# Modulation in two column halves, keys and queries side by side, and four V tiles in the first block of a transformer layer

## The chip, the cores and the metric

The kernel runs on one core of a Trainium2 chip. The metric is the device time of one execution in microseconds; the kernel before takes 1766.52 us, the median of three runs (1766.45 to 1767.83). A core has five engines that run side by side, each through its own list of instructions in order: TensorE (PE, with its weight loads shown as PEld), VectorE (DVE), ScalarE (ACT), GpSimd (POOL) and SyncE (SP), which here only issues DMAs. They wait for each other through semaphores.

## The reference

One transformer layer with conditional modulation, in fp32, for 2048 tokens of width 512:

```
mod = silu(c) @ w_mod                      # six vectors of 512: sa, ca, ga, sb, cb, gb
h   = layernorm(x) * (1 + ca) + sa
q, k, v = h @ wqkv                         # 32 heads of 16
x   = x + ga * (softmax(q k^T / 4) v @ wo)
h   = layernorm(x) * (1 + cb) + sb
x   = x + gb * (gelu(h @ w1 + b1) @ w2 + b2)
```

The inner width of the last step is 1792. Only the beginning matters here: the vectors `ca` and `sa`, the first layer norm, and the projections of its output to keys, queries and values.

## The kernel before

**Numbers in two parts.** Each fp32 operand of a projection is split into a high part, rounded to the format in which TensorE runs fast, and a low part, the remainder. A product is three matmuls per chunk of 128 features: high by high, low by high, high by low. A tile of 512 output columns over four chunks is therefore 12 matmuls, all into one PSUM bank (`mm3`, L294).

**Blocks.** The 2048 tokens are four blocks of 512. For each block b the loop at L534 gives out, in this order: the layer-norm statistics of block b+1 (`ln1`, L271), the load of x for block b+2, the key projection of head group 0 (`proj_qk`, L307), the normalisation of the rows of block b+1 (L278, DVE), the query projection, then some V tiles (`proj_v`, L354), the transposes of block b+1 with their evacuation (`ln1_t`, L284; `transposed`, L252), more V tiles, and in blocks 0 and 1 two further modulation vectors (`mod_rows`, L205). `V_A` (L47) says how many V tiles stand before and behind the transposes: 1 and 2 in block 0, 1 and 1 in block 1, 0 and 1 in block 2. The remaining ten V tiles and all other head groups follow behind the blocks, then attention, then the feed-forward part. There is no planner: the order of each engine's work is the order in which the Python code gives it out.

**Evacuating the transposes.** The transposed normalised x of a chunk lies in PSUM as 128 features by 512 tokens. ACT scales and shifts it by two columns of `modc` (one plus `ca`, and `sa`, per feature; L262) into an fp32 tile, DVE rounds that to `hi` (L263), and DVE or POOL, in turn, subtracts to get `lo` (L264).

**Before the first block.** SP loads c, the four tiles of x of block 0, two 1 MB tables of `w_mod` (for `ca` and `sa`), the weights of the first keys and queries, the V weights, x of block 1 and the second group's weights, in this order. PE first runs 22 throwaway matmuls on an identity matrix (`keep_warm`, L509, `NWARM`); then `mod_part` (L200) multiplies silu(c) with the first table, the chunks of x are transposed, the second table is multiplied, five throwaway matmuls follow, and `mod_cols` (L216) turns the row of 512 values (copied from PSUM by ACT, `mod_copy`) into columns, by four matmuls of two columns each, from which DVE writes `modc`. Only then can the evacuation begin. `split_w` (L164) splits the weights: those of group 0 on DVE with one subtraction on POOL, the V weights on ACT with subtractions in turn on DVE and POOL. POOL sets the constant columns of five V staging tiles (L503 to L505) right behind the layer norm's power of -0.5 (L241).

**Pairs of blocks.** In odd blocks the keys of the two last blocks are also added and subtracted (L330, DVE), rounded (L331, ACT) and their remainders taken on POOL (L346).

**PSUM.** Eight banks are dealt out from three rings: `mx` (three banks), `sc` (four) and `pv` (one). A bank can be dealt again once its last reader is done.

Of the kernel before, what the change touches and what calls it, by code (L numbers as in the profile page):

```python
# [7 lines left out]
F32 = mybir.dt.float32  # L8
# [8 lines left out]
P = 128  # L17
# [35 lines left out]
def block_kernel(ctx: ExitStack, tc: tile.TileContext, x, wqkv, wo, w1, b1, w2, b2, c, w_mod, out):  # L53
# [78 lines left out]
    sel_b = apool.tile([P, 2, P], F32, name="sel_b")  # L132
    ones = apool.tile([P, 2 * S // P], F32, name="ones")
    gp.memset(ones, 1.0)

    wm_r = w_mod.rearrange("(k p) n -> p k n", p=P)

    def load_wm(i, slot):
        sy.dma_start(halves[1][slot], wm_r[:, :, i * D : (i + 1) * D])
        return halves[1][slot]  # L140

    def x_tile(b, t):
# [10 lines left out]
    def load_w(k):  # L153
# [7 lines left out]
                sy.dma_start(raw[:, i], wq_r[:, i, 2 * D :])  # L161
        raws[k] = raw

    def split_w(k):  # L164
        raw = raws.pop(k)
        if k < 4:
            t = wslots[k % 2].rearrange("p a (b n) -> p (a b) n", n=P).rearrange("p (h w k) n -> p h w k n", h=2, w=2)
            for w in (1, 0):
                if k == 0:
                    ve.tensor_copy(t[:, 0, w], raw[:, w])  # L170
                elif k > 1:
                    gp.tensor_copy(t[:, 0, w], raw[:, w])
                else:
                    ac.activation(t[:, 0, w], raw[:, w], AF.Copy)
                eng = ve if k == 0 and w else gp
                eng.tensor_tensor(t[:, 1, w], raw[:, w], t[:, 0, w].bitcast(F32), op=ALU.subtract)
            w_hi[k], w_lo[k] = t[:, 0], t[:, 1]
        else:
            w_hi[k], w_lo[k] = vslots
            for i in range(KC):  # L180
                ac.activation(w_hi[k][:, i], raw[:, i], AF.Copy)
                eng = gp if i % 2 else ve
                eng.tensor_tensor(w_lo[k][:, i], raw[:, i], w_hi[k][:, i].bitcast(F32), op=ALU.subtract)

    sy.dma_start(c_c, c.rearrange("a (k p) -> p (a k)", p=P))
    load_x(0)
    wms = [load_wm(1, 0), load_wm(0, 1)]
    load_w(0)


    ac.activation(s_c, c_c, AF.Exp, scale=-1.0)
# [8 lines left out]
    def mod_part(ps, i, wm):  # L200

        for k in range(KC):
            te.matmul(ps[32 * k : 32 * (k + 1)], s_m[:, i, k], wm[:, k], start=i == 0, stop=i == 1)

    def mod_rows(wms):  # L205
        ps = bank()
# [1 line left out]
            mod_part(ps, i, wms[i])  # L208
        return mod_copy(ps)

    def mod_copy(ps):
        r = apool.tile([P, D], F32, tag="h32", name="mrow", bufs=3)
        ac.activation(r, ps, AF.Copy)
        return r

    def mod_cols(v, r):  # L216

        ps = bank()
        for fc in range(KC):
            te.matmul(ps[:, fc * 2 : fc * 2 + 2], r[:, fc * P : (fc + 1) * P], sel[:, :2], start=True, stop=True)  # L220
        p2 = ps[:, : 2 * KC].rearrange("p (f i) -> p f i", i=2)
        ve.tensor_scalar(modc[:, v, :, 0], p2[:, :, 0], 1.0, None, op0=ALU.add)
        ve.tensor_copy(modc[:, v, :, 1], p2[:, :, 1])

    def mod_store(r):

# [77 lines left out]

    st = [ac]

    def proj_qk(b, k, w, fill=()):  # L307
        hi, lo = hT[b]
        ps = bank()
        mm3(ps, [w_hi[k][:, w, i] for i in range(KC)], [w_lo[k][:, w, i] for i in range(KC)],  # L310
            [hi[:, i] for i in range(KC)], [lo[:, i] for i in range(KC)], fill)
        parts = tpool.tile([P, 2, TB], FR, tag="parts", name="parts", bufs=5)
        pair = w and k < 2
        if k or pair and b % 2 == 0:
            raw = tpool.tile([P, TB], F32, tag="raw", name="raw", bufs=3)
            ac.activation(raw, ps, AF.Copy)
            if pair:
                k2[b % 2] = raw
        if k:
            gp.tensor_copy(parts[:, 0], raw)  # L320
            gp.tensor_tensor(parts[:, 1], raw, parts[:, 0].bitcast(F32), op=ALU.subtract)
        else:
            ac.activation(parts[:, 0], ps, AF.Copy)
            ve.tensor_tensor(parts[:, 1], ps, parts[:, 0].bitcast(F32), op=ALU.subtract)
        if pair and b % 2:
            pm = [tpool.tile([P, TB], F32, tag="pm", name="pm", bufs=1), k2[0]]
            pmh = [tpool.tile([P, 2, TB], FR, tag="parts", name="pmh", bufs=5) for _ in range(2)]
            if not k:
                for i, op in enumerate((ALU.add, ALU.subtract)):
                    ve.tensor_tensor(pm[i], ps, k2[0], op=op)  # L330
                    ac.activation(pmh[i][:, 0], pm[i], AF.Copy)  # L331

        def pair_store():
            for i in range(2):
                t0 = (b - 1 + i) * TB
                st[0].dma_start(kpm_d[k][:, :, t0 : t0 + TB].rearrange("a p t -> p a t"), pmh[i].bitcast(F32))

        def rest():
            st[0].dma_start(qk_d[w][k][:, :, b * TB : (b + 1) * TB].rearrange("a p t -> p a t"), parts.bitcast(F32))
            if pair and b % 2:  # L340
                for i, op in enumerate((ALU.add, ALU.subtract)):
                    if k:
                        gp.tensor_tensor(pm[i], k2[1], k2[0], op=op)
                        gp.tensor_copy(pmh[i][:, 0], pm[i])
                    eng = ve if not k and b == NB - 1 else gp
                    eng.tensor_tensor(pmh[i][:, 1], pm[i], pmh[i][:, 0].bitcast(F32), op=ALU.subtract)  # L346
# [7 lines left out]
    def proj_v(b, t, fill=()):  # L354
        hi, lo = hT[b]
        ps = bank()
        sl = slice(t * P, (t + 1) * P)
        mm3(ps, [hi[:, i, sl] for i in range(KC)], [lo[:, i, sl] for i in range(KC)],
            [w_hi[4][:, i] for i in range(KC)], [w_lo[4][:, i] for i in range(KC)], fill, late_b=False)
# [134 lines left out]
        return [] if left[u] else [max_rows(u)]  # L494


    load_w(4)
    load_x(1)
    load_w(1)
    sy.dma_start(one_d.rearrange("a (p f) -> (a p) f", p=P // 2), ones)  # L500
    xn = ln1(0)()
    for t in vst:
        gp.memset(t[:, :, 4 * VW :], 0.0)  # L503
        for j in range(4):
            gp.memset(t[:, :, j * VW + DH], 1.0)  # L505
    split_w(0)
    warm = bank_pv()

    def keep_warm(n):  # L509
        for i in range(n):  # L510
            te.matmul(warm[:, :P], ident, ident, start=True, stop=True)

    keep_warm(NWARM)
    ps = bank()
    mod_part(ps, 0, wms[0])
    ev = ln1_t(0, xn, lambda: mod_part(ps, 1, wms[1]))
    mrow = mod_copy(ps)
    keep_warm(5)
    mod_cols(0, mrow)
    ev()  # L520
    split_w(4)
    wms = [load_wm(4, 0), load_wm(3, 1)]
    mrow = None
    vitems = [(b, t) for b in range(NB) for t in range(4)]
# [9 lines left out]
    for b in range(NB):  # L534
        if b == NB - 1:
            close(lcm)
            kcm, kpool = pool("kpool")
            kts = [kpool.tile([P, 2, S], FR, name=f"kt{i}") for i in range(2)]
            qmcm, qmpool = pool("qmpool")
            kpm[0], kpm[1] = kts  # L540
            load_qm(0)
        if b + 1 < NB:
            rows = ln1(b + 1)
        if b + 2 < NB:
            load_x(b + 2)
        proj(proj_qk, b, 0, 1)
        if b == NB - 1:
            st[0] = sy
            rest()
            rest, st[0] = lambda: None, ac  # L550
            build_k(kts[0], kpm_d[0], 0, 0, 2 * TB)
            split_w(1)
            load_w(2)
        else:
# [470 lines left out]
```

## Time and profile before

| | |
|---|---|
| median of three runs | 1766.52 us (1766.45 to 1767.83) |
| profiled execution | 1765.35 us, span 1763.6 us |
| PE busy | 1748.7 us, 99% of the span |
| DVE, ACT, POOL busy | 1404.5, 1355.8, 320.1 us |
| mean granted clock of TensorE | 0.998 |
| DMA traffic | 144.17 MB, mean 82 GB/s |

The profile is one execution. Its times are microseconds from the first instruction. A timeline line shows start, duration, engine, source line, operation, output and inputs by the program's names, shapes and the number of instructions put together; in square brackets the idle time of the engine before it, and what ended it. An fp32 matmul appears as two records, a transpose as one. "PEclk" is the share of its full clock that TensorE was granted. A line of the windows view has the stretch, its length, then the busy time and number of instructions of PE, PEld, DVE, ACT and POOL, the granted clock, the share of the DMA engines that was busy, and GB/s.

### The profile page before, as it was taken

To read this page: it belongs to the slowest core of one execution; us is meant where nothing else is said; L and a number is where in the kernel's file an instruction comes from. 1 tells how busy PE (TensorE), PEld (TensorE's weight loads), DVE (VectorE), ACT (ScalarE), POOL (GpSimd) and SP (SyncE) were. 2 spreads that over 40 slices of the span, in tenths; PEclk is the share of its full clock that TensorE was granted. 3 is DMA by queue.
4 is the path that set the end of the run, shared out by engine and by line. 5 is a ranking of instruction groups with operands and counts; after the bars stand their busy time and mean duration, and the time that the engine had idled before them with its cause. 6 is when DMAs were issued, how large, how long until landed. Compare 5 with 4: busy or idle time off the path is not lost.

```text
span 1763.6 us, 29164 instructions
## 1 busy us (share of the span) xinstructions
PE 1748.7 (99%) x10554; PEld 901.1 (51%) x10554; DVE 1404.5 (80%) x2553; ACT 1355.8 (77%) x2580; POOL 320.1 (18%) x347
## 2 busy tenths in 40 slices
PE   8999999999999999999999999999999999999998
PEld 6755555344343443343343343343433478788887
DVE  6579999898888888888888888888886286838453
ACT  3478888999999999999999999999999732213222
POOL 3204422010000000000000000000003154636462
PEclk9999999999999999999999999999999999999999
DMA  8767636811500411411410101101013064423341
GB/s 277 250 141 163 151 115 130 130 37 29 87 23 23 82 27 23 74 36 23 74 35 24 38 25 33 38 23 36 23 60 104 22 195 131 126 78 114 102 120 48
DMA packets 124100, 144.17 MB, mean 82 GB/s; under 512 B 38930, under 2 KB 72722, under 8 KB 122004
## 3 DMA queue, kind: packets, MB, share of 16 engines
q1 hardware_dynamic: 120644, 135.55, 30.9%
q10 hardware_dynamic: 3312, 6.76, 1.0%
q8 instruction: 83, 1.36, 0.3%
q14 instruction: 61, 0.50, 0.1%
HBM read 106.37 MB, written 35.87 MB: 81 GB/s over the span
## 4 chain that ended last, share of the span: by engine, by line
PE 93%; DVE 3%; DMA 1%; issue 1%; POOL 1%; SPq 0%; ACT 0%; ACTq 0%; DVEq 0%; POOLq 0%
PE pv L693 29%; PE mx L429 19%; PE sc L300 16%; PE sc L860 13%; PE mx L447 6%; PE mx L924 5%; PE pv L924 2%; PE sc L800 1%; PE mx L800 1%; DMA wmod<-in_w_mod_dram 1%; DVE glo L907 0%; POOL w2l L731 0%; DMA rb<-rden 0%; PE sc L257 0%; DVE mxs L431 0%
## 5 line engine op out<-in xcount | busy, mean ns | idle before, releaser
L861 ACT ACTIVATE p<-sc 128x512 f32<-128x512 f32 x2048 | 1054.8, 615 | 39.4 <-PE sc L860 13.4
L431 DVE TENSOR_REDUCE mxs<-mx 128x1 f32<-128x512 f32 x1472 | 927.5, 684 | 112.9 <-PE sc L860 76.6
L693 PE MATMUL pv<-p,vg 128*32 128x512 f32 x4096 | 546.0, 605 | 0.0
L860 PE MATMUL sc<-qst,kq 50*128 50x512 f32 x1024 | 284.1, 435 | 0.0
L860 PE MATMUL sc<-qst,kt 50*128 50x512 f32 x1024 | 282.3, 431 | 0.0
L429 PE MATMUL mx<-kq,qmx 48*128 48x512 f32 x768 | 262.1, 428 | 0.2
L429 PE MATMUL mx<-kt,qmx 48*128 48x512 f32 x704 | 240.3, 428 | 0.1
L429 PEld LDWEIGHTS mx<-kq,qmx 48*128 48x128 f32 x768 | 122.6, 184 | 228.5 <-DVE mxs L431 209.2
L903 ACT ACTIVATE g<-sc,b_c 128x512 f32<-128x512 f32 x56 | 38.6, 690 | 237.2 <-PE sc L300 233.1
L429 PEld LDWEIGHTS mx<-kt,qmx 48*128 48x128 f32 x704 | 113.3, 184 | 208.8 <-DVE mxs L431 191.1
L458 DVE CUSTOM_DVE_ANT_0 cp<-mx,cp 128x512 f32<-128x512 f32 x288 | 187.2, 688 | 36.3 <-PE mx L447 31.3
L471 POOL CAST m<-mn 128x16 fp32r<-128x16 f32 x32 | 6.3, 197 | 1026.0 <-DVE mn L465 1026.0
L454 ACT ACTIVATE cp<-mx 128x512 f32<-128x512 f32 x288 | 156.3, 597 | 38.8 <-PE mx L447 38.4
L693 PEld LDWEIGHTS pv<-p,vg 128*32 128x32 f32 x4096 | 81.1, 108 | 180.7 <-issue 169.3
L860 PEld LDWEIGHTS sc<-qst,kq 50*128 50x128 f32 x1024 | 125.5, 185 | 32.1 <-ACT p L861 23.6
L907 DVE TENSOR_TENSOR glo<-g,ghi 128x512 fp32r<-128x512 f32 x56 | 60.1, 1073 | 94.8 <-ACT ghi L906 94.8
L860 PEld LDWEIGHTS sc<-qst,kt 50*128 50x128 f32 x1024 | 125.5, 185 | 10.1 <-ACT p L861 3.1
L447 PE MATMUL mx<-kt,qmx 48*128 48x512 f32 x576 | 113.4, 455 | 0.0
L729 POOL TENSOR_TENSOR w1l<-w1r,w1h 128x512 fp32r<-128x512 f32 x56 | 76.8, 1372 | 152.7 <-DVE w1h L728 130.5
L447 PEld LDWEIGHTS mx<-kt,qmx 48*128 48x128 f32 x576 | 58.3, 184 | 56.4 <-issue 33.4
L300 PE MATMUL sc<-hThi,w 128*128 128x512 f32 x256 | 84.0, 436 | 2.2 <-DVE hThi L263 2.2
L731 POOL TENSOR_TENSOR w2l<-w2r,w2h 128x512 fp32r<-128x512 f32 x56 | 81.1, 1448 | 6.6 <-DVE w2h L730 6.2
(158 smaller groups left out, 1671.4 us busy)
## 6 DMA issues: line engine op xcount, KB each, us to landing
w1r<-in_B_w_dram SPq DMA_DIRECT2D x56, 256.0 KB
w2r<-in_B_w_dram SPq DMA_DIRECT2D x56, 256.0 KB
qk<-parts SPq DMA_DIRECT2D x25, 512.0 KB
qmx<-qk SPq DMA_DIRECT2D x192, 64.0 KB
qst<-qk SPq DMA_DIRECT2D x192, 64.0 KB
wmod<-in_w_mod_dram SPq DMA_DIRECT2D x6, 1024.0 KB
kq<-qk SPq DMA_DIRECT2D x24, 256.0 KB
kt<-qk SPq DMA_DIRECT2D x24, 256.0 KB
```

What stands on the lines that cost most here:

```text
L300: te.matmul(ps, p, q, start=i == 0, stop=i == len(terms) - 1)
L429: te.matmul(ps, qmx[u][rows, p, qc * P : (qc + 1) * P], kst[u // NB][rows, p, kr * TB : (kr + 1) * TB], start=True, stop=True)
L431: ve.tensor_reduce(mxs[u][:, p, a, qc, kr : kr + 1], ps, axis=AX.X, op=ALU.max, negate=True)
L447: te.matmul(ps, qmx[u][rows, p, qc * P : (qc + 1) * P], kpm[u // NB][rows, p, t0 : t0 + TB], start=True, stop=True)
L454: ac.activation(vabs[n, a], ps, AF.Abs)
L458: ve.tensor_tensor_reduce(v, ps, v, -0.5, 3.0e38, ALU.add, ALU.min, mxs[u][:, p, a, qc, r : r + 1])
L693: te.matmul(cur_pv[0][32 * j : 32 * (j + 1)], vg[g][:, kc, j * VW : j * VW + 32], pt.pop((s, j)), start=kc == 0, stop=kc == NKC - 1)
L729: gp.tensor_tensor(alo, a, ahi.bitcast(F32), op=ALU.subtract)
L731: gp.tensor_tensor(blo, b, bhi.bitcast(F32), op=ALU.subtract)
L860: te.matmul(ps, k[r0 : r0 + KX, p, kc * P : (kc + 1) * P], q[r0 : r0 + KX, p], start=True, stop=True)
L861: ac.activation(pb, ps, AF.Exp, scale=SCALE)
L924: te.matmul(acc[qb][t], p[:, sl], q, start=f == 0 and n == 0, stop=f == NF - 1 and n == 2)
```

## The change

A function `first_block` takes the place of the code before the loop and of block 0's two projections.

- Each of the two `w_mod` tables is loaded in two halves of 256 columns: first halves, then the first key and query weights, then second halves. The load of the second group's weights (`load_w(1)`) goes from the start into block 1.
- `mod_part`, `mod_copy` and `mod_cols` work on a half. The first half gives the columns of `modc` for feature chunks 0 and 1, the second those for chunks 2 and 3.
- PE's throwaway matmuls become 34, 8, 6 and 4 at four places, for 22 and 5.
- The transposes go row tile by row tile over all four chunks, where they went chunk by chunk.
- ACT writes the rounded `hi` and the fp32 copy straight from PSUM, by two activations; DVE subtracts. POOL has no part in it.
- Keys and queries of block 0 have a bank each and are accumulated chunk by chunk: high-high and low-high for chunks 0 and 1, then high-low for these, then the same for chunks 2 and 3.
- The first weights are rounded on ACT and subtracted on DVE. The V weights are rounded two on DVE and two on ACT, and subtracted two on DVE and two on POOL, behind the block's evacuation.
- POOL sets the staging tiles' constants before its other work. The rows of block 1 are normalised behind both projections of block 0.
- `V_A` becomes 3 and 1 in block 0, 0 and 1 in block 1, 0 and 1 in block 2. The first V tile multiplies by the low weights last.

```diff
-NWARM = 22
+NWARM = 34
-V_A = ((1, 2), (1, 1), (0, 1))
+V_A = ((3, 1), (0, 1), (0, 1))
...
+    for t in vst:
+        gp.memset(t[:, :, 4 * VW :], 0.0)
...
-    wms = [load_wm(1, 0), load_wm(0, 1)]
+    wms = [load_wm(1 - i, i, 0, HD) for i in range(2)]
     load_w(0)
+    for i in range(2):
+        load_wm(1 - i, i, HD, D)
+    load_w(4)
+    load_x(1)
...
+    def first_block(tiles):
...
+        keep_warm(NWARM)
+        mod_part(mod, 0, wms[0], 0, HD)
+        keep_warm(8)
+        mod_part(mod, 1, wms[1], 0, HD)
+        ac.activation(w_hi[0][:, 1], raw[:, 1], AF.Copy)
+        mrow = mod_copy(mod, None, 0, HD)
+        ac.activation(w_hi[0][:, 0], raw[:, 0], AF.Copy)
+        keep_warm(6)
+        tr(0)
+        mod_cols(0, mrow, cols, 0, 2)
+        for t in range(1, 4):
+            tr(t)
+        for w in (1, 0):
+            sub(w_lo[0][:, w], raw[:, w], w_hi[0][:, w])
+        put(hi[:, 0], 0)
+        put(hi[:, 1], 1)
+        mod_part(mod, 0, wms[0], HD, D)
+        keep_warm(4)
+        mm("hh", 0)
+        mod_part(mod, 1, wms[1], HD, D)
+        mod_copy(mod, mrow, HD, D)
+        mm("hh", 1)
+        mm("lh", 0)
+        mod_cols(0, mrow, cols, 2, 4)
+        mm("lh", 1)
+        hs = {}
+        for f0 in (0, 2):
+            if f0:
+                for fc in (2, 3):
+                    put(hi[:, fc], fc)
+                for i in (0, 1):
+                    ve.tensor_copy(w_hi[4][:, i], vr[:, i])
+            for fc in (f0, f0 + 1):
+                hs[fc] = apool.tile([P, TB], F32, tag="h32", name="h32", bufs=3)
+                put(hs[fc], fc)
+                sub(lo[:, fc], hs[fc], hi[:, fc])
+            if f0:
+                mm("hh", 2, 3)
+                mm("lh", 2, 3)
+            mm("hl", f0, f0 + 1)
+        for i in (2, 3):
+            ac.activation(w_hi[4][:, i], vr[:, i], AF.Copy)
+        for i in range(KC):
+            sub(w_lo[4][:, i], vr[:, i], w_hi[4][:, i], gp if i > 1 else ve)
+        return acc
...
-        proj(proj_qk, b, 0, 1)
+        proj(proj_qk, b, 0, 1, (), None if b else first[1])
+        if b == 1:
+            load_w(1)
...
-        else:
+        elif b:
             xn = rows()
-        proj(proj_qk, b, 0, 0)
+        proj(proj_qk, b, 0, 0, (), None if b else first[0])
+        if b == 0:
+            xn = rows()
...
-            proj(proj_v, *vitems.pop(0))
+            proj(proj_v, *vitems.pop(0), (), len(vitems) == 15)
```

`mm(kind, *fcs)` gives out, for each chunk, one matmul into the keys' bank and one into the queries'. `put(dst, fc)` is ACT's eviction with scale and shift. `sub` is a subtraction on DVE unless an engine is named.

More of the change, by code (lines that the diff above doesn't have):

```diff
@@ L198, in block_kernel, with mod_part @@
     gp.tensor_copy(sel_b, sel[:, :2, None].to_broadcast([P, 2, P]))
-    def mod_part(ps, i, wm):
+    def mod_part(ps, i, wm, c0=0, c1=D):
         for k in range(KC):
-            te.matmul(ps[32 * k : 32 * (k + 1)], s_m[:, i, k], wm[:, k], start=i == 0, stop=i == 1)
+            te.matmul(ps[32 * k : 32 * (k + 1), c0:c1], s_m[:, i, k], wm[:, k, c0:c1], start=i == 0, stop=i == 1)
     def mod_rows(wms):
@@ L209, in mod_rows, with mod_copy, mod_cols @@
         return mod_copy(ps)
-    def mod_copy(ps):
-        r = apool.tile([P, D], F32, tag="h32", name="mrow", bufs=3)
-        ac.activation(r, ps, AF.Copy)
-        return r
-    def mod_cols(v, r):
-        ps = bank()
-        for fc in range(KC):
+    def mod_copy(ps, r=None, c0=0, c1=D):
+        if r is None:
+            r = apool.tile([P, D], F32, tag="h32", name="mrow", bufs=3)
+        ac.activation(r[:, c0:c1], ps[:, c0:c1], AF.Copy)
+        return r
+    def mod_cols(v, r, ps=None, f0=0, f1=KC):
+        if ps is None:
+            ps = bank()[:, : 2 * KC]
+        for fc in range(f0, f1):
             te.matmul(ps[:, fc * 2 : fc * 2 + 2], r[:, fc * P : (fc + 1) * P], sel[:, :2], start=True, stop=True)
-        p2 = ps[:, : 2 * KC].rearrange("p (f i) -> p f i", i=2)
-        ve.tensor_scalar(modc[:, v, :, 0], p2[:, :, 0], 1.0, None, op0=ALU.add)
-        ve.tensor_copy(modc[:, v, :, 1], p2[:, :, 1])
+        p2 = ps.rearrange("p (f i) -> p f i", i=2)
+        ve.tensor_scalar(modc[:, v, f0:f1, 0], p2[:, f0:f1, 0], 1.0, None, op0=ALU.add)
+        ve.tensor_copy(modc[:, v, f0:f1, 1], p2[:, f0:f1, 1])
     def mod_store(r):
@@ L305, in block_kernel, with keep_warm, tr, put @@
     st = [ac]
-    def proj_qk(b, k, w, fill=()):
+    def first_block(tiles):
+        hi = hpool.tile([P, KC, TB], FR, name="hThi0")
+        lo = hpool.tile([P, KC, TB], FR, name="hTlo0")
+        hT[0] = hi, lo
+        raw, vr = raws.pop(0), raws.pop(4)
+        w_parts(0)
+        w_hi[4], w_lo[4] = vslots
+        warm = bank_pv()
+        cols = warm[:, P : P + 2 * KC]
+        mod = bank()
+        xT = [bank_mx() for _ in range(KC - 1)] + [bank()]
+        acc = {w: bank() for w in (1, 0)}
+        def keep_warm(n):
+            for i in range(n):
+                te.matmul(warm[:, :P], ident, ident, start=True, stop=True)
+        def tr(t):
+            for fc in range(KC):
+                te.transpose(xT[fc][:, t * P : (t + 1) * P], tiles[t][:, fc * P : (fc + 1) * P], ident)
+        def put(dst, fc):
+            ac.activation(dst, xT[fc], AF.Identity, scale=modc[:, 0, fc, 0:1], bias=modc[:, 0, fc, 1:2])
+        def mm(kind, *fcs):
+            for fc in fcs:
+                for w in (1, 0):
+                    p, q = {"hh": (w_hi, hi), "lh": (w_lo, hi), "hl": (w_hi, lo)}[kind]
+                    te.matmul(acc[w], p[0][:, w, fc], q[:, fc], start=kind == "hh" and fc == 0,
+                              stop=kind == "hl" and fc == KC - 1)
+        def sub(dst, a, b, eng=ve):
+            eng.tensor_tensor(dst, a, b.bitcast(F32), op=ALU.subtract)
+        keep_warm(NWARM)
[10 more added lines that the diff above has]
+            tr(t)
+        for w in (1, 0):
+            sub(w_lo[0][:, w], raw[:, w], w_hi[0][:, w])
[30 more added lines that the diff above has]
+        return acc
@@ L308, in proj_qk @@
+    def proj_qk(b, k, w, fill=(), ps=None):
         hi, lo = hT[b]
[L309 to L311 removed]
+        if ps is None:
+            ps = bank()
+            mm3(ps, [w_hi[k][:, w, i] for i in range(KC)], [w_lo[k][:, w, i] for i in range(KC)],
+                [hi[:, i] for i in range(KC)], [lo[:, i] for i in range(KC)], fill)
         parts = tpool.tile([P, 2, TB], FR, tag="parts", name="parts", bufs=5)
@@ L494, in next_max @@
         return [] if left[u] else [max_rows(u)]
[L497 to L521, printed above, removed]
+    first = first_block(ln1(0)())
     wms = [load_wm(4, 0), load_wm(3, 1)]
```

39 lines of the change are left out of this document (17 added, 22 removed).

## Prediction

> **What bounds the kernel now.** I read the page first, then the chain of waits over the first 80 us, then each engine's timeline there, and last the windows for the granted clock.
>
> ```profile
> span 1763.6 us, 29164 instructions
> PE 1748.7 (99%) x10554; PEld 901.1 (51%) x10554; DVE 1404.5 (80%) x2553; ACT 1355.8 (77%) x2580; POOL 320.1 (18%) x347
> PE 93%; DVE 3%; DMA 1%; issue 1%; POOL 1%; SPq 0%; ACT 0%; ACTq 0%; DVEq 0%; POOLq 0%
> ```
>
> PE carries 93% of the chain, so behind the change every microsecond of delay on PE is one of the end. The diff leaves the work after block 2 as it is: six V tiles are done by then in both kernels (1+2, 1+1, 0+1 before; 3+1, 0+1, 0+1 after). So only the first 56 us count. PE's timeline there:
>
> ```profile
> 1.35 7.25 PE L511 MATMUL pv<-ident 128*128 128x128 f32 x44 [1.35 <-POOL mhalf L110]
> 10.96 1.06 PE L203 MATMUL sc<-wmod,s_m 128*32 128x512 f32 x8 [2.36 <-DVE xin L278]
> 11.96 1.62 PE L257 MATMUL mx<-ident,xin 128*128 128x128 f32 x12
> ...
> 15.18 1.28 PE L511 MATMUL pv<-ident 128*128 128x128 f32 x10
> 16.30 0.95 PE L220 MATMUL sc<-sel,mrow 128*128 128x2 f32 x8
> 18.84 0.78 PE L300 MATMUL sc<-hThi,w 128*128 128x512 f32 x2 [1.60 <-DVE hThi L263]
> ...
> 28.32 2.03 PE L300 MATMUL sc<-wv,hThi 128*128 128x512 f32 x8
> 30.19 1.09 PE L300 MATMUL sc<-wv,hTlo 128*128 128x512 f32 x4
> 31.12 1.47 PE L257 MATMUL mx<-ident,xin 128*128 128x128 f32 x12
> ...
> 38.56 1.92 PE L203 MATMUL sc<-wmod,s_m 128*32 128x512 f32 x16
> 40.42 2.12 PE L300 MATMUL sc<-hThi,w 128*128 128x512 f32 x8
> ...
> 46.02 0.95 PE L220 MATMUL sc<-sel,mrow 128*128 128x2 f32 x8
> 46.83 2.11 PE L300 MATMUL sc<-wv,hThi 128*128 128x512 f32 x8
> ...
> 49.72 1.48 PE L257 MATMUL mx<-ident,xin 128*128 128x128 f32 x12
> ...
> 56.22 2.12 PE L300 MATMUL sc<-hThi,w 128*128 128x512 f32 x8
> ```
>
> The first block's key and query projections run from 18.84 to 28.32: 9.5 us for 24 matmuls. A V tile's 12 take 28.32 to 31.12, 2.80 us, so 24 could take 5.6. The windows tell why they don't:
>
> ```profile
> 9.00:12.50 3.50, 1.54 (x12) 0.62 (x13) 3.02 (x4) 0.00 (x0) 1.68 (x26) 1.00 1.07 375
> 15.90:19.40 3.50, 1.90 (x15) 1.56 (x14) 1.38 (x5) 1.85 (x3) 1.26 (x1) 1.00 1.08 371
> 19.40:22.80 3.40, 2.83 (x6) 1.66 (x6) 3.37 (x7) 3.06 (x6) 1.90 (x2) 0.50 1.10 356
> 22.80:26.20 3.40, 3.40 (x9) 2.64 (x8) 3.33 (x7) 0.97 (x2) 3.40 (x3) 0.50 1.05 389
> ```
>
> The clock (third number from the end) falls to 0.50 at 19.4, after a stretch in which PE did eight two-column matmuls and then waited 1.60 us, and returns at 26.2: 6.8 us at half speed.
>
> **The change, part by part.** Time to the end of the first block, step by step on PE, in the order of the new program. A 128x128 fp32 matmul is two records, and ten records start within 16.30-15.18, so 0.112 each; a transpose is one record of 0.109 (12 in 31.12 to 32.43).
>
> The warm-up grows from 22 to 34 matmuls: 24 more records, 2.7 us. The first 44 end at 8.60, and a record outlasts the next one's start by 0.16 (1.28 less nine times 0.112 is 0.27, less 0.11): next start 8.4+2.7 = 11.1. A modulation half has half the columns of the 1.0 us group at 10.96, between 0.5 and 1.0; I take 0.5, for the columns halve and nothing else does. Then: half 11.6, 8 warm (1.8) 13.4, half 13.9, 6 warm (1.35) 15.25, four transposes 15.7, two column products (0.45) 16.15, twelve transposes 17.45, half 17.95, 4 warm 18.85. The data for this are there:
>
> ```profile
> 3.67 9.98 DMA wmod<-in_w_mod_dram
> ```
>
> The whole second table landed at 13.65, with 3.15 MB of x and tables ahead of and in it. The second half-table now has 2.1 MB: pro rata from 2.3 us, 9.9 us. PE reaches it at 13.4, so even no gain at all in landing costs 0.3. SP issues two more DMAs of 0.5 us, in front of loads that wait for the wire. The w1 load leaves this queue for block 1, where nobody asks for it before block 3; it costs nothing.
>
> ```profile
> 14.82 0.60 ACT L213 ACTIVATE mrow<-sc 128x512 f32<-128x512 f32 x1 [11.63 <-PE sc L203]
> 17.55 2.12 ACT L262 ACTIVATE h<-mx,modc 128x512 f32<-128x512 f32 x3 [2.13 <-DVE modc L223]
> 9.30 3.02 DVE L278 TENSOR_SCALAR xin<-xin,mv,rs 128x512 f32<-128x512 f32 x4 [1.22 <-POOL rs L241]
> 14.55 0.43 DVE L170 CAST w<-wraw 128x512 fp32r<-128x512 f32 x1 [2.23 <-DMA wraw<-in_A_wqkv_dram]
> 17.29 0.16 DVE L222 TENSOR_SCALAR modc<-sc 128x4 f32<-128x4 f32 x1 [1.24 <-PE sc L220]
> 18.82 0.69 DVE L264 TENSOR_TENSOR hTlo<-h,hThi 128x512 fp32r<-128x512 f32 x1
> ```
>
> The raw key weights landed at 14.5 in the old order; their rounding goes from DVE (0.43) to ACT (as the eviction of 14.82, 0.60 each, between 12 and 15.7 however they land), and both low parts stay on DVE, 0.69 each, behind the first `modc` (16.4, two columns' products and 0.25 as at 17.29): 17.9, where PE asks at 20.3. Hidden; were the weights 3 us late, PE would wait for them one for one. Three evictions of activations take 2.12, 0.68 apiece. The first `hi` chunk follows the last transpose, 17.4 to 18.2, before PE asks at 18.85. From there PE goes in pairs of 0.47: hh0 19.3, half 19.8, hh1 and lh0 20.75, two column products 21.2, lh1 21.65. The fp32 copy of chunk 0 (ACT, from 20.4) is ready, but DVE writes `modc` first (21.6), so `lo` 0 ends at 22.3 and `lo` 1 at 22.9: hl0, hl1 end at 23.4. ACT's four evictions of chunks 2 and 3 run 21.7 to 24.5 and the last `lo` ends at 25.2; PE does six pairs 23.4 to 26.2 without a stop. **First block: 26.2 for 28.32, 2.1 us gained**, with the clock at full speed because PE has something at all times. Moving the memsets ahead takes up to 1.1 us out of the 3.02 of row 9.30 (the same group takes 1.92 at 29.04, below), hidden by the longer warm-up.
>
> Behind it, DVE and POOL split the V weights (DVE rounds two of the four chunks, 0.43 each, while it waits for ACT's evictions; ACT the others behind them), then x of block 1 is normalised:
>
> ```profile
> 20.22 1.66 DVE L264 TENSOR_TENSOR hTlo<-h,hThi 128x512 fp32r<-128x512 f32 x1
> 22.13 2.37 DVE L183 TENSOR_TENSOR wv<-vraw,wv 128x512 fp32r<-128x512 f32 x2
> 24.42 0.68 DVE L236 BATCH_NORM_STATS2 bst<-xin 128x6 f32<-128x512 f32 x1
> 27.82 0.68 DVE L324 TENSOR_TENSOR parts<-sc,parts 128x512 fp32r<-128x512 f32 x1
> 29.04 1.92 DVE L278 TENSOR_SCALAR xin<-xin,mv,rs 128x512 f32<-128x512 f32 x4 [0.54 <-POOL rs L241]
> 46.06 3.87 DVE L278 TENSOR_SCALAR xin<-xin,mv,rs 128x512 f32<-128x512 f32 x4
> ```
> ```profile
> 19.93 1.39 POOL L264 TENSOR_TENSOR hTlo<-h,hThi 128x512 fp32r<-128x512 f32 x1 [2.54 <-DVE hThi L263]
> ...
> 46.16 1.59 POOL L346 TENSOR_TENSOR pmh<-pm,pmh 128x512 fp32r<-128x512 f32 x1 [4.87 <-ACT pmh L331]
> 47.70 1.48 POOL L346 TENSOR_TENSOR pmh<-raw,pmh 128x512 fp32r<-128x512 f32 x1
> ```
>
> DVE's two subtractions of V weights take 2.4 (row 22.13) to 3.3 (twice 1.66, each beside one of POOL's). The Trainium skill's page "SBUF — State Buffer" (The single rule) says why: VectorE and GpSimd hold their shared port pair for a whole instruction and the other blocks. Row 20.22 agrees, with 1.66 for 0.69; by that rule the four would be done one after the other, the upper end here. I take 3.0. The statistics to the first `parts` subtraction last 27.82-24.42 = 3.4, itself 0.7: 25.2+3.0+3.4+0.7 = 32.3. The third V tile takes the bank that this frees. PE's first two tiles end at 31.8, and the first waits for the last low weights: together between 0 and 1.6 of stall, **I take 0.8**.
>
> The fourth V tile lies ahead of block 1 now: **+2.80**. In block 1 it is missing between 46.83 and 49.72. There the transposes follow the column products at once and wait for the normalised rows, which DVE does from 46.06 to 49.93 whatever PE does, slowed to 3.87 from 1.92 by POOL's subtractions (46.16 to 49.18). The last row comes 9.5 us after block 1 begins (40.42), in both kernels. So PE idles 3.0 us where it did the tile, and gets back some **0.1**. This term carries the forecast: the tile filled a hole there, and fills none where it stands now, but for what the stall of 0.8 would be without it.
>
> That hole has a second price. Two-column matmuls of 0.95 and 3.0 idle are longer than the stretch at 16.30 (0.95 and 1.60) that cost the clock. If one window of 3.4 us goes by at half speed, half of it is lost, **1.7**; with the 6.8 us of 19.4 to 26.2, 3.4; without any, 0. The stretch of 9.00 to 12.50, PE busy 1.54, did not cost the clock, so none is possible; I take one window.
>
> Sum: -2.1 +0.8 +2.8 -0.1 +1.7 = **+3.1 us**. The profiled execution took 1765.35 (1.75 around its span) and would take 1768.45; the median of the three runs stands 1.17 higher, at 1766.52. I add the sum to that: **1769.6**.
>
> **The rivals.**
> No clock loss in the hole: +1.4, 1767.9. For it: the row of 9.00 to 12.50. Against it: that of 15.90 to 19.40, with more PE busy and a loss all the same. The page "TensorE: Matmul & The Clock Gate" of the Trainium skill (Why this matters for your kernels) warns of idle gaps over some 3 us, one idle window of 3.4; by that rule a 3.0 us hole just passes, and the sum is 1767.9. The trace does not bear the rule out in this form, for 1.60 wholly idle was enough at 17.25.
>
> Two windows lost, as at 19.4: +4.8, 1771.3, slower. It decides if the drop falls before the hole ends, since a window that is partly idle does not bring the clock back (19.40 to 22.80, PE busy 2.83 of 3.40, stayed at 0.50).
>
> The half clock comes in the first block too: its four column products, transposes and short waits might count as idleness as at 16.30. 24 matmuls at 0.43 for 0.23 are 4.7, about 3 of it in one window and a half: +6, 1772.5. Against it: nowhere in the new order does PE stand still over 0.6 us.
>
> The hole closes: should POOL's two subtractions come later than DVE's rows, these take 1.92, the hole is 1.1 and keeps the clock: 1.4-1.9 = -0.5, 1766.0. Against it: their order on the queues is that of before. To be faster by over 0.2% (3.5 us, about what a measurement of this kernel tells from no change) the first block would have to end at 21 as well, sooner than its warm-ups and evictions let it.
>
> **How the numbers follow.** One window lost 0.42, own range 1768.0 to 1771.0 (the stalls of 0 to 1.6, and as much again for the first block's chain), a third of it beyond +3.5; no loss 0.26; two windows 0.17; the first block at half clock 0.08; hole closed 0.07, of which, with all the rest mispriced too, 0.05 is for faster. Slower: 0.14+0.17+0.08 = 0.39, rounded 0.40; same 0.55; faster 0.05. Range 1766.0 to 1772.5, from the closed hole to the half clock in the first block.
>
> **What would show it.** In the profile after: the first matmul of block 1's keys near 41.8 (40.42 before); the first block's last matmul near 26.2 at clock 1.00 throughout; the first transposes of block 1 idle some 3 us for DVE's rows of 3.9 us; the clock at 0.50 for about 3.4 us from there; block 2's keys 3 us later than at 56.22. Wrong it would be by a first block much shorter than worked out, by rows of 1.9 us in block 1, or by a drop of the clock elsewhere.

## The result and the profile after

The changed kernel takes 1771.05 us, the median of nine runs (1768.29 to 1783.95), beside 1766.96 us for the kernel before (nine runs, 1766.2 to 1767.89): a ratio of 1.0034, 95% interval 1.0021 to 1.0048. The change makes the kernel slower; by the medians it loses 4.1 us. (A ratio counts long executions too, here those of 1780.33 and 1783.95, which lift it above the 1.0023 of the two medians; of all the runs below it leaves out one, at 1792.88.) The profiled execution took 1770.16 us, 4.81 more than that of before. The page of the changed kernel begins:

```profile
span 1768.4 us, 29298 instructions
PE 1755.2 (99%) x10620; PEld 907.1 (51%) x10620; DVE 1402.0 (79%) x2554; ACT 1358.8 (77%) x2585; POOL 315.8 (18%) x344
```

PE is as full as it was, and busy 6.5 us longer. Its timeline, which answers to the one shown of before:

```profile
1.36 9.46 PE L330 MATMUL pv<-ident 128*128 128x128 f32 x68 [1.36 <-POOL mhalf L110]
10.75 0.64 PE L207 MATMUL sc<-wmod,s_m 128*32 128x256 f32 x8
...
19.04 0.72 PE L343 MATMUL sc<-hThi,w 128*128 128x512 f32 x2
19.68 0.64 PE L207 MATMUL sc<-wmod,s_m 128*32 128x256 f32 x8
...
22.70 1.34 PE L343 MATMUL sc<-hTlo,w 128*128 128x512 f32 x4 [0.34 <-DVE hTlo L347]
...
26.61 0.40 PE L306 MATMUL sc<-wv,hThi 128*128 128x512 f32 x1
...
33.07 2.13 PE L306 MATMUL sc<-wv,hThi 128*128 128x512 f32 x8 [0.24 <-DVE parts L413]
...
42.46 2.12 PE L306 MATMUL sc<-hThi,w 128*128 128x512 f32 x8
...
50.10 0.33 PE L263 MATMUL mx<-ident,xin 128*128 128x128 f32 x1 [0.92 <-DVE xin L284]
51.50 2.13 PE L263 MATMUL mx<-ident,xin 128*128 128x128 f32 x10 [1.07 <-DVE xin L284]
...
54.13 2.94 PE L306 MATMUL sc<-wv,hThi 128*128 128x512 f32 x8
...
59.79 2.12 PE L306 MATMUL sc<-hThi,w 128*128 128x512 f32 x8
```

The first V matmul, which marks the end of the first block, starts at 26.61, where it was 28.32. Block 1's keys start at 42.46 (40.42), block 2's at 59.79 (56.22): 3.57 us are lost by there. In block 1 the transposes follow the column products and wait for the normalised rows, 0.92 and 1.07 us. The eight high-weight matmuls of the V tile behind them take 2.94 us, where the others take 2.1. The windows give the clock (third number from the end):

```profile
19.40:22.80 3.40, 3.06 (x21) 1.75 (x19) 0.98 (x4) 2.41 (x5) 0.00 (x0) 1.00 1.01 338
22.80:26.20 3.40, 3.40 (x15) 2.60 (x16) 3.09 (x6) 3.11 (x6) 0.73 (x1) 1.00 0.96 346
50.00:53.40 3.40, 2.10 (x11) 1.72 (x12) 2.64 (x6) 0.00 (x0) 1.16 (x1) 0.87 1.02 359
53.40:56.80 3.40, 3.40 (x14) 2.89 (x13) 0.96 (x2) 1.80 (x3) 0.00 (x0) 0.62 1.08 393
```

The half-clock stretch of the first block is gone, and one of about 3.4 us stands at the hole of block 1. On the other engines (DVE, then POOL, then ACT; an ACTq row is a DMA that ACT issues from its own list):

```profile
16.43 1.28 DVE L347 TENSOR_TENSOR w<-wraw,w 128x512 fp32r<-128x512 f32 x2
...
25.51 3.50 DVE L347 TENSOR_TENSOR wv<-vraw,wv 128x512 fp32r<-128x512 f32 x2
...
32.33 1.28 DVE L413 TENSOR_TENSOR parts<-sc,parts 128x512 fp32r<-128x512 f32 x2
...
48.10 3.81 DVE L284 TENSOR_SCALAR xin<-xin,mv,rs 128x512 f32<-128x512 f32 x4
```
```profile
25.47 3.00 POOL L347 TENSOR_TENSOR wv<-vraw,wv 128x512 fp32r<-128x512 f32 x2 [15.52 <-ACT wv L390]
...
48.20 1.56 POOL L435 TENSOR_TENSOR pmh<-pm,pmh 128x512 fp32r<-128x512 f32 x1 [2.23 <-ACT pmh L420]
```
```profile
49.97 4.98 ACTq L425 DMA_DIRECT2D kpm<-pmh  x2
54.99 2.12 ACT L268 ACTIVATE h<-mx,modc 128x512 f32<-128x512 f32 x3 [5.66 <-DMA v<-vst]
```

DVE's rows start with POOL's remainders and take 3.81. ACT's evictions start only at 54.99, behind the two stores of the key sums, the second of which waited for the landing of a V store.

Behind block 2 the profiled execution loses another 1.24 us (4.81 less 3.57). PE waits there, in the feed-forward part, in both kernels alike. First the kernel before, PE's timeline and the window behind the wait, then the changed one, the same two views:

```profile
1526.03 0.50 PE L924 MATMUL mx<-w2h,glo 128*128 128x512 f32 x1 [2.25 <-DVE glo L907]
```
```profile
1527.00:1530.40 3.40, 3.40 (x16) 2.81 (x16) 3.33 (x7) 0.00 (x0) 0.73 (x2) 1.00 0.93 313
```
```profile
1529.45 0.50 PE L993 MATMUL mx<-w2h,glo 128*128 128x512 f32 x1 [2.24 <-DVE glo L976]
```
```profile
1530.40:1533.80 3.40, 3.40 (x10) 2.70 (x9) 3.33 (x7) 0.00 (x0) 0.74 (x2) 0.52 0.83 281
```

The same wait, 2.25 and 2.24 us, cost nothing of the clock in one execution and a window at half speed in the other. Ahead of that window the changed kernel is 3.42 us behind (1529.45 for 1526.03), so the rest is lost from there on. Among the fourteen profiled executions of this document the clock fell at this wait in four.

### The profile page after: what moved, and what is told of

It reads as the page before. It is cut to its first block, busy times and chain, and to the rows that moved or that the text cites. A ratio compares the mean times of both kernels' runs of the same rounds, so it can differ in the third digit from the quotient of the medians.

```text
span 1768.4 us, 29298 instructions
## 1 busy us (share of the span) xinstructions
PE 1755.2 (99%) x10620; PEld 907.1 (51%) x10620; DVE 1402.0 (79%) x2554; ACT 1358.8 (77%) x2585; POOL 315.8 (18%) x344
## 4 chain that ended last, share of the span: by engine, by line
PE 93%; DVE 3%; issue 1%; POOL 1%; DMA 1%; ACT 0%; SPq 0%; ACTq 0%; POOLq 0%; DVEq 0%
PE pv L762 29%; PE mx L518 20%; PE sc L306 15%; PE sc L929 13%; PE mx L536 6%; PE mx L993 5%; PE pv L993 2%; PE sc L869 1%; PE pv L330 1%; PE mx L869 1%; DVE glo L976 0%; POOL w2l L800 0%; PE sc L263 0%; DMA rb<-rden 0%; PE sc L207 0%
## 5 line engine op out<-in xcount | busy, mean ns | idle before, releaser
L306 PE MATMUL sc<-hThi,w 128*128 128x512 f32 x240 | 77.3, 428 | 0.0
```

What stands on the lines that cost most here:

```text
L306: te.matmul(ps, p, q, start=i == 0, stop=i == len(terms) - 1)
```

## The experiments

The theory: the fourth V tile, moved out of block 1, leaves a hole there and costs the time, and the hole costs a clock window on top. Rivals: the new first block or its side effects cost it, or the moved load of the second group's weights does.

**The tile alone, both ways.** First the changed kernel with the tile back in block 1, then the kernel before with only the tile moved:

```diff
-V_A = ((3, 1), (0, 1), (0, 1))
+V_A = ((3, 0), (1, 1), (0, 1))
```


> The changed kernel with V tiles 3+0 in block 0, 1+1 in block 1, 0+1 in block 2: the fourth tile goes back to block 1, ahead of its transposes. Theory (the moved tile opens the hole in block 1, and the hole costs the clock): block 1's keys can begin some 2.8 us earlier but wait for their operands, whose last part came at 42.8 in the changed kernel, so they end near 43.3 instead of 45.5; from there block 1 goes as before (12.8 us to block 2's keys), which start near 56.1 instead of 59.8; no idle of PE at block 1's transposes; time 3 to 4 us below the changed kernel, near the kernel before. Rival (the first block, its warm-ups and its V weights carry the loss): within 1 us of the changed kernel.


```diff
-V_A = ((1, 2), (1, 1), (0, 1))
+V_A = ((1, 3), (0, 1), (0, 1))
```


> The kernel before with one edit: V tiles 1+3 in block 0 and 0+1 in blocks 1 and 2, so the tile that stood ahead of block 1's transposes is done in block 0. Theory: block 1's keys start 2.8 us later (43.2 for 40.42), PE idles 3.0 us at block 1's transposes, block 2's keys come 2.7 us later than 56.22, and 1.7 more if the clock drops for one window: 2.7 to 4.4 us slower than the kernel before. Rival (a tile that is moved costs nothing, for the sum of the work is the same): within 0.5 us of the kernel before.

With the tile back: 1767.38 us (11 runs, 1766.54 to 1769.19), ratio to before 1.0002 (0.9993 to 1.0011); 3.7 us less than the changed kernel by the medians. With only the tile moved: 1770.09 us (10 runs, 1768.44 to 1775.1), ratio 1.0021 (1.0012 to 1.003). PE's timeline with the tile back, then with only the tile moved:

```profile
40.03 1.66 PE L306 MATMUL sc<-hThi,w 128*128 128x512 f32 x6
42.15 0.73 PE L306 MATMUL sc<-hThi,w 128*128 128x512 f32 x2 [0.46 <-DVE hThi L269]
...
57.48 2.12 PE L306 MATMUL sc<-hThi,w 128*128 128x512 f32 x8
```
```profile
43.35 2.12 PE L300 MATMUL sc<-hThi,w 128*128 128x512 f32 x8
...
50.99 0.33 PE L257 MATMUL mx<-ident,xin 128*128 128x128 f32 x1 [0.92 <-DVE xin L278]
52.39 1.66 PE L257 MATMUL mx<-ident,xin 128*128 128x128 f32 x10 [1.07 <-DVE xin L278]
...
59.08 2.12 PE L300 MATMUL sc<-hThi,w 128*128 128x512 f32 x8
```

The move alone makes the same hole in the old kernel, with the same two waits, and puts block 2's keys at 59.08, 2.86 later than at 56.22; in this execution no clock was lost there (the ten transposes take 1.66, not 2.13). So the moved tile is the loss, whichever first block stands ahead of it. The first fence says where the first block's gain went: with the tile back, block 1's keys start only 0.39 earlier than at 40.42 and wait for their operands; block 1 lasts 17.45 us (40.03 to 57.48) for 15.80. DVE and ACT are not ready for a PE that comes sooner. Block 2's keys are 1.26 us later than before in this execution, where 56.1 was expected, although the medians are level.

**The hole's second price.** The changed kernel with eleven throwaway matmuls in the hole, which give PE something to do and move nothing else:

```diff
         if b == 1:
             mod_cols(1, mrow)
+            warm = bank_pv()
+            for _ in range(11):
+                te.matmul(warm[:, :P], ident, ident, start=True, stop=True)
```


> The changed kernel with 11 throwaway matmuls (22 records of 0.112, 2.5 us) between block 1's column products and its transposes, where PE idled. Theory (the idle hole itself costs the clock): clock 1.00 around the hole, block 2's keys near 58.1 instead of 59.8, 1.7 us below the changed kernel, and if the long losses of clock in some executions start there too, no execution above 1772. Rival (the drop has another cause, and the matmuls only push the transposes back): the same time as the changed kernel or up to 0.5 us more, with the same spread.

1769.24 us (11 runs, 1768.12 to 1773.45), ratio 1.0012 (1.0003 to 1.002): 1.8 less than the changed kernel by the medians. One execution is above 1772, where none was expected. PE's timeline:

```profile
43.19 2.12 PE L306 MATMUL sc<-hThi,w 128*128 128x512 f32 x8
...
49.60 2.70 PE L633 MATMUL pv<-ident 128*128 128x128 f32 x22
...
58.93 2.12 PE L306 MATMUL sc<-hThi,w 128*128 128x512 f32 x8
```

From block 1's keys to block 2's it is 15.74 us, for 17.33 in the changed kernel: 1.59, about half a window of 3.4. The granted clock is 1.00 from 43 to 57 us here, and nothing else of the program changed, so that was the clock. Not every execution pays it: in the profiled ones of the kernel with only the tile moved, above, and of one below the clock held through the same waits.

**The hole closed at its source.** DVE's rows are slow while POOL subtracts. Here POOL's two remainders of the pair go to DVE, behind its rows:

```diff
-                    eng = ve if not k and b == NB - 1 else gp
+                    eng = ve if not k else gp
```


> The changed kernel with the two subtractions of block 1's key sums and differences on DVE, behind its rows, instead of on POOL, beside them. Theory: DVE's four rows take 1.9 us instead of 3.8, the hole in block 1 shrinks from 3.0 us to 1.1, the clock stays up, block 2's keys near 56.3: 3.6 us below the changed kernel (1.9 if the clock still drops). Rival (the rows don't bound the transposes): no difference.

1770.34 us (12 runs, 1767.74 to 1785.39), ratio 1.0019 (1.001 to 1.0028): 0.7 less than the changed kernel by the medians, where 3.6 was expected. The profiled execution is the slowest of the twelve, for a reason that lies behind block 2 (see the end). DVE, PE and ACT in turn:

```profile
48.40 1.91 DVE L284 TENSOR_SCALAR xin<-xin,mv,rs 128x512 f32<-128x512 f32 x4
```
```profile
49.17 2.39 PE L263 MATMUL mx<-ident,xin 128*128 128x128 f32 x12
...
56.59 0.73 PE L306 MATMUL sc<-hThi,w 128*128 128x512 f32 x2
57.53 1.19 PE L306 MATMUL sc<-hThi,w 128*128 128x512 f32 x4 [0.21 <-DVE hThi L269]
59.89 0.74 PE L306 MATMUL sc<-hThi,w 128*128 128x512 f32 x2 [1.17 <-DVE hThi L269]
60.48 0.86 PE L306 MATMUL sc<-hTlo,w 128*128 128x512 f32 x3
```
```profile
51.58 3.54 ACTq L425 DMA_DIRECT2D kpm<-pmh  x2
55.17 2.12 ACT L268 ACTIVATE h<-mx,modc 128x512 f32<-128x512 f32 x3 [5.54 <-PE sc L306]
```

The rows fall from 3.81 to 1.91 and the hole is gone, so POOL beside DVE made it. But ACT's evictions start at 55.17 all the same, behind its key-sum stores, and PE now waits for them in block 2. The stop had been hidden behind the hole.

**What holds ACT's stores.** The suspect was the load of the second group's weights, which the change put where these stores are. Two kernels have it under `b == 2` in place of `b == 1`, one with DVE's remainders and one with the tile back:

> The kernel with the two subtractions on DVE, and the load of the second group's weights moved on from block 1 to block 2. There the rows took 1.9 us, but ACT's evictions for block 2 began only at 55.2, behind its store of the key sums, which waited 3.5 us for the landing of an earlier V store on a busy wire. Theory (with the hole closed, that store is what is late next, and the moved load put it there): the store goes out within 2 us, ACT's first eviction starts near 52.5, block 2's keys near 56.3 without the 1.4 us of waits inside them; 1.5 to 2 us below the kernel with the load in block 1 (1770.3 median, 1769.3 where the clock stayed up). Rival (the load is hidden wherever it stands, as the prediction had it): no difference.

> The kernel with V tiles 3+0, 1+1, 0+1, and the load of the second group's weights moved on from block 1 to block 2. Both theories: here the same store took 1.8 us, ACT's evictions waited for the transposes, so within 0.5 us of that kernel (1767.4). A gain of over 1 us would mean that the load costs by the wire and not by the store's wait.

1772.89 us (6 runs, 1768.18 to 1784.66; ratio 1.0041, 1.0019 to 1.0064) and 1767.79 us (4 runs; ratio 1.0005, 0.9992 to 1.0017). This tells nothing of the load: SP's list of DMAs is the same with and without the edit, since no other issue lies between the two places. These are repeats of the kernels without it. The edit that does move the load puts it back to the start:

```diff
     load_w(4)
     load_x(1)
+    load_w(1)
...
-        if b == 1:
-            load_w(1)
```


> The changed kernel with the second group's weights loaded at the start again, behind x of block 1, as in the kernel before; SP's queue is the place that differs (a move from block 1 to block 2 in the source, tried in two earlier kernels, left SP's list as it was). If the moved load is hidden, as the prediction has it, block 2's keys start at 59.8 as in the changed kernel and the time stays near 1770 to 1771. If its 0.5 MB, which are on the wire from 47.6 when the second key-sum store waits on ACT's queue for the landing of a V store, are what holds this store to 54.6, the store goes 1 to 2 us earlier and ACT's evictions start at about 53.6, which the transposes of 53.4 to 54.5 then set: no gain in PE's time here, but V tile and modulation stay where they are. If the load at the start delays the first x or tables, the first block ends later than 26.6.

> The kernel with the pair remainders on VectorE, with the second group's weights loaded at the start. Here the evictions could begin at 52.1, when the transposes are in, and begin at 55.2 since the second key-sum store is issued at 54.75. If the weights' load holds the V store on the wire, it is issued at about 52.5 to 53.5, the evictions begin 1 to 2 us earlier, and the waits for hThi of 0.21 and 1.17 in block 2's keys go: 1.2 to 1.6 us off its 1769 to 1770. If the wire is held by x of block 3 and the modulation tables, the store stays at 54.5 to 54.8 and the time with it.

On the changed kernel: 1771.18 us (10 runs, 1768.36 to 1774.21), ratio 1.0021 (1.0012 to 1.003). On the one with DVE's remainders: 1769.81 us (10 runs, 1766.32 to 1789.54), ratio 1.003 (1.0005 to 1.0055). ACT's queue in the first, then ACT and PE in the second:

```profile
50.74 1.80 ACTq L426 DMA_DIRECT2D kpm<-pmh  x2
53.27 2.12 ACT L269 ACTIVATE h<-mx,modc 128x512 f32<-128x512 f32 x3 [2.99 <-PE mx L264]
```
```profile
51.76 0.97 ACTq L426 DMA_DIRECT2D kpm<-pmh  x2
52.77 2.12 ACT L269 ACTIVATE h<-mx,modc 128x512 f32<-128x512 f32 x3 [2.96 <-DVE modc L230]
```
```profile
56.77 2.12 PE L307 MATMUL sc<-hThi,w 128*128 128x512 f32 x8
58.73 1.08 PE L307 MATMUL sc<-hTlo,w 128*128 128x512 f32 x4
```

The two stores take 1.80 and 0.97 us on the queue in place of 4.98 and 3.54. So the load's place did hold them. In the second kernel the keys' waits of 0.21 and 1.17 are gone: from its first matmul to the low parts block 2's keys need 1.96 us (56.77 to 58.73), for 3.89 (56.59 to 60.48). The time does not show it: 1.2 to 1.6 us were expected, the medians differ by 0.5, and long executions (1779.01 to 1789.54, three of ten) make the interval wide. In the changed kernel itself the load's place costs nothing that the medians show: there PE stands at the hole anyway, its first block began later in this execution (see the end), and the clock held. The same waits of 0.92 and 1.07 stand in its trace, and block 1 takes 15.71 us by PE's timeline:

```profile
43.41 2.12 PE L307 MATMUL sc<-hThi,w 128*128 128x512 f32 x8
...
59.12 2.12 PE L307 MATMUL sc<-hThi,w 128*128 128x512 f32 x8
```

**What the longer warm-up costs.** The kernel with the tile back and 22, then 26, then again 22 throwaway matmuls at the start in place of 34; last with 22 and the load at the start:

> The kernel with V tiles 3+0, 1+1, 0+1, and 22 warm-up matmuls at the start instead of 34. Theory (the chain of the first block hangs on the warm-ups, since PE reached each half-table after it had landed): the first half's matmuls begin at 8.5 to 9.5 instead of 10.75, the first block ends near 24.8 instead of 26.6, DVE's work behind it moves along, block 2's keys 1.5 to 2.3 us earlier: 1765.1 to 1765.9, below both kernels. Rival (the tables' landing holds the chain, the warm-ups only fill a wait): the first block ends at 26.6 with idle PE ahead of the second half, same time, or up to 1.7 us more if the clock is lost for it.

> The changed kernel with the fourth V tile back in block 1 and 26 warm-ups of two matmuls ahead of the first half-table where it has 34. By the theory that the change's gain lies in the first block and its loss in the moved tile, the start before the first half-table shrinks by 8 x 0.278 = 2.2 us of warm-ups, of which the landing of the half-table (read at 9.10 where only 22 warm-ups stood, with a wait of 0.30) leaves all but about 0.5 usable: the half-table is read at about 9.1, block 2's keys start near 55.1, and the time is that of 22 warm-ups where the clock stays up, 1765 to 1766.5 us. The difference to 22 warm-ups is only that no idle time is left before the half-table; if idle time there were what costs some executions their clock, the runs here would hold 0.998 to 0.999 and none would be near 1770; if not, about two in five runs would again be at 0.996 and 1770 us.

> The same kernel as the one with the fourth V tile back in block 1 and 22 warm-ups, for more runs of it: by the trace before (block 2's keys at 55.05 against 56.22 in the kernel before, 1.2 us earlier) the median should be 1765.5 to 1766.5 us where the clock holds and ratio 0.999 to 1.000; if the two runs at 1770 us were its normal share, the median stays near 1766 to 1767 and the interval takes in no change.

> The kernel with the fourth V tile back in block 1 and 22 warm-ups, with the second group's weights loaded at the start: by the reading that this load is hidden in either place, block 2's keys at 55.0 and 1764.5 to 1766 us, no difference to the same kernel without the move beyond 1 us. If the 0.5 MB at the start delay the modulation tables or x of block 2, a wait for them shows ahead of block 1 and it is later by up to 1.4 us, the load's time on the wire.

| kernel | median (runs) | ratio to before |
|---|---|---|
| 22 | 1766.19 (5, to 1770.58) | 1.0003 (0.9991 to 1.0015) |
| 26 | 1767.56 (12, 1764.24 to 1792.88) | 1.0007 (0.9989 to 1.0025) |
| 22, repeated | 1765.39 (11, 1764.37 to 1769.01) | 0.9991 (0.9982 to 0.9999) |
| 22, load at the start | 1764.62 (11, 1763.71 to 1769.57) | 0.9992 (0.9984 to 1.0001) |

PE's timeline with 22, the first time:

```profile
9.10 0.64 PE L207 MATMUL sc<-wmod,s_m 128*32 128x256 f32 x8 [0.30 <-DMA wmod<-in_w_mod_dram]
...
55.05 1.20 PE L306 MATMUL sc<-hThi,w 128*128 128x512 f32 x4
```

The first half-table is there at 9.1, so the 12 added matmuls hold PE back 1.65 us (10.75 in the changed kernel less 9.10), and without them block 2's keys start at 55.05, ahead of 56.22 before and of 57.48 with 34. With 26, PE waits for nothing ahead of the half-table in the profiled execution, and still five of the twelve are at 1769.47 or above, two of them at 1783.92 and 1792.88: so executions lose time without the short wait that 22 leave there. The last kernel has the lowest median of all, 6.4 us under the changed one and 2.7 under before, by the median of the executions of before that were taken with it (1767.29). Its interval just takes in no change, that of 22 repeated just leaves it out: a gain over the kernel before is at the edge of what can be told.

## Why the prediction was right and wrong

The time, 1771.05, lies in the range and 1.45 us above the 1769.6 forecast: 0.44 of that is the kernel before, which came out at 1766.96 for 1766.52, the rest the loss, 4.09 by the medians where the sum was 3.1. What was wrong is the side: no change was called likelier than slower. The terms of the sum against PE's rows:

| step | forecast | measured |
|---|---|---|
| first block | -2.1 (26.2) | -1.71 (26.61 for 28.32) |
| fourth tile and stalls | +2.80 and +0.8 | +3.75 (42.46 less 26.61, for 12.10) |
| block 1 | -0.1 and +1.7 | +1.53 (17.33 for 15.80) |
| by block 2's keys | +3.1 | +3.57 |
| behind block 2 | 0 | +1.24 in the profiled execution; the medians leave some 0.5 (4.09 less 3.57), whose place no run shows |

**Right:** the moved tile as the term that carries it; the hole at block 1's transposes, made by rows of 3.8 us beside POOL; one clock window of 3.4 us lost there, 1.6 to 1.8; the first block at full clock throughout; the first half-table read at 10.75, forecast for 11.1. The waits in the hole are 0.92 and 1.07, not 3.0 in one piece: the transposes of the rows that are ready run between them.

**Wrong, the bound.** This is the step that put the forecast on the wrong side. The prediction set a loss of up to 3.5 us equal to no change, "about what a measurement of this kernel tells from no change", and so most of the chance of its own +3.1 fell to no change. The measurements tell smaller differences than that. The changed kernel's interval reaches 0.0013 to 0.0014 to either side of its ratio, about 2.4 us, and that of the kernel with eleven throwaway matmuls (1.0003 to 1.002) leaves no change out at a loss of 2 us (1769.24 for 1767.29). With such a bound the prediction's own sum says slower.

**Wrong in kind:** "So only the first 56 us count", which put everything behind block 2 at nothing. The work behind block 2 is the same, but not its clock: the wait of 2.24 us in the feed-forward part cost a window in the profiled execution of after and none in that of before. The sum had no term for this, of either sign, and stood 0.4 under the bound. Whether the clock is lost there more often after the change than before is not shown.

**Wrong in size, first block:** PE reaches the parts of the chain later than worked out. From its start to the next, a modulation half took 0.57 (19.68 to 20.25), not 0.5, four times, and the first pair 0.64 (19.04 to 19.68), not 0.47. So the second columns of `modc` are late, and the low parts that follow them on DVE release PE at 22.70, where the chain had 22.3. DVE's two subtractions of V weights took 3.50, above the 2.4 to 3.3 allowed; the subtraction that frees the third tile's bank starts at 32.33 and lets that tile start at 33.07, where 32.3 was forecast. By the rule of the Trainium skill's page "SBUF — State Buffer" (Who interferes with whom), the port pair that DVE and POOL share is locked by one of them at a time, and a DVE instruction with two inputs in SBUF needs it. The trace agrees: two such subtractions take 3.50 on DVE beside POOL's two of 3.00, and two take 1.28 at 16.43, where POOL does nothing.

The gain of 1.71 is also a fortunate one. The V matmul that ends the first block starts at 26.61 in this execution, at 26.90 to 27.56 in the seven other profiled executions with 34 throwaway matmuls at the start.

**Wrong, though it cost nothing here:** that the moved load "costs nothing" because nobody asks for it before block 3. It lies on the wire ahead of a V store, this holds ACT's key-sum stores, and these hold the evictions until 54.99. What hid it is the hole, as the kernel without the hole showed.

**Of the rivals,** a hole that keeps its clock did occur in two profiled executions with the same waits, but the median pays the window, as the eleven throwaway matmuls show. That the hole closes was rightly given little: POOL's subtractions came with DVE's rows.

## What to carry to other kernels

Work that PE does while another engine is late is free only where it stands: before moving it, look at what it covers, and at what is late behind that (here rows, then ACT's stores, then operands of the next block). A DMA that nobody needs soon still takes the wire from a store for which an engine's queue stands still. Work out from the spread of many runs what size of change can be told from none: here 2 us could, and the forecast's bound was 3.5. When a forecast sum lies next to that bound, price the clock in the stages that the change doesn't touch as well. And see in each engine's list that an edit really moved something.

## What the runs showed of the hardware

**The clock falls at short waits, and not in every execution.** It fell after 0.92 and 1.07 us of waiting, with transposes between, and after 2.24; it held through the same waits in other executions. The Trainium skill's page "TensorE: Matmul & The Clock Gate" (Part 1: The HAM clock gate) has the activity window run freely, not started by the kernel; that agrees with a loss that comes and goes. Its rule of one whole idle window of about 3.4 us does not agree: none of these waits was that long.

**A long stretch at half speed with PE busy.** In two profiled executions, of the two kernels with DVE's remainders, which took 1785.39 and 1781.49 us, the clock fell near 100 us and stayed at 0.50, for about 34 us in the first and 37.5 in the second. A window of the first:

```profile
103.00:120.00 17.00, 17.00 (x46) 7.79 (x45) 10.00 (x31) 8.98 (x18) 0.00 (x0) 0.50 0.78 109
```

It begins where matmuls of 48 rows take turns with V tiles. Ahead of it PE waited once for ACT, 0.42 and 0.23 us, and in the changed kernel's profile a wait of 0.17 at the same place cost nothing. A stretch of 34 us at half speed is worth about 17 us, and the slowest runs of five kernels stand 12 to 25 us over their medians; the changed kernel is one of them (1780.33, 1783.95). No profile of the changed kernel caught one, so for it this is a guess, and the cause is open: nothing was run that takes that wait away.

**The warm-up itself varies.** The same 68 records at the start took 9.46 us in the changed kernel (above) and 10.41 in the one with the load at the start:

```profile
1.36 10.41 PE L331 MATMUL pv<-ident 128*128 128x128 f32 x68 [1.36 <-POOL mhalf L110]
```

PE's records come slowly at first, and for longer in the second: from 1.40 to 5.00 us PE did 18 records in the changed kernel and 17 in the other, from 5.00 to 9.00 it did 39 and 30. The granted clock reads 1.00 in all four stretches, so in the first microseconds that column does not tell the pace of PE's records. The V matmul that marks the first block's end starts at 27.56 there, 0.95 later than at 26.61. A start that waits for data, as with 22 of them, hides as much of such a difference as it waits (0.30 us in the row above); one that waits for its own warm-up hides nothing.
